# A fused Fourier, dense MoE and routed MoE kernel: one PSUM rotation, generators paced by TensorE's work, and a Fourier stage laid evenly over the chunks

## Chip, cores and metric

The kernel runs on one core of a Trainium2 chip. The metric is device time in microseconds (us), the median of several runs. Engines are named as in the profile: PE is TensorE, DVE VectorE, ACT ScalarE, POOL GpSimd, SP SyncE.

## The reference

Three stages follow each other: a filter in the frequency domain along the sequence, a gated MLP behind an RMS norm, and a top-1 mixture of experts. Eight batches of 3072 tokens with 256 features.

```python
def _attn_ref(x, w_r, w_i, b_r, b_i):
    X = np.fft.rfft(x, axis=1)
    Yr = Xr @ w_r - Xi @ w_i + b_r
    Yi = Xr @ w_i + Xi @ w_r + b_i
    Yr = np.sign(Yr) * np.maximum(np.abs(Yr) - lam, 0.0)   # Yi likewise
    return np.fft.irfft(Yr + 1j * Yi, n=x.shape[1], axis=1)
...
def _moe_ref(x, w_gate, w_val, w_out, rms_g):
    xn = x / np.sqrt(np.mean(x * x, axis=-1, keepdims=True) + 1e-06) * rms_g
    g = xn @ w_gate
    return (g * (1.0 / (1.0 + np.exp(-g))) * (xn @ w_val)) @ w_out      # d_ff 1536
...
def _moe2_ref(x, expert_emb, tau, w1, w2):                               # 8 experts, F 1024
    logits = normed(x) @ normed(expert_emb).T / tau
    expert_idx = np.argmax(logits, axis=1)
    # gate_w: the softmax of the logits at that expert
    out[mask] = gate_w[mask, None] * (np.maximum(x[mask] @ w1[e], 0.0) @ w2[e])
```

## The kernel before

The 24,576 tokens are cut into 64 chunks of 384 tokens, eight (c0 to c7) in each of eight batches. There are four stages: a start with the Fourier stage of batch 0 and the weights' preparation; seven batches whose chunks carry, in between, the Fourier stage of the next batch; batch 7, which carries the preparation of expert weights instead; and `phase_C`, the routed experts. Products are made of fp16 pairs (a high and a low part), three matmuls for one.

The work of a chunk is two runs of matmuls on PE. First, `gv` (L870) makes twelve gate and value tiles: for each f, six matmuls of 384 columns into a gate tile and six into a value tile (L879). ACT takes Silu of the gate tile into `th`, DVE multiplies it with the value tile into `hf`, which is then split into `hh` (ACT) and `hl` (DVE). Second, `out_tile` (L905) makes three output tiles of 36 matmuls with 264 columns (L913); the last 8 columns are routing logits.

Three other strands are written as Python generators, and calls in `gv` and in the main loop place their steps between these matmuls:

- `norm_steps` (L808) for the next chunk: 24 matmuls (L819) of the last Fourier step from `gt`, which was loaded from DRAM; squares on ACT; sums `q`, `q`, `ql` on POOL; a sum over features on PE (L839); a Newton reciprocal root on DVE; and `xnh`, `xnl`. `tick` takes one step at each call.
- `route_steps` (L928) for the chunk before: argmax, a prefix count on PE (L967, L969), positions, three scatters of row numbers `idl` by indirect DMA on POOL (L984), gate weights (`d`, `se`, `gw`), and a row written to DRAM.
- `gen_A` (L377), the Fourier stage of the next batch. In its A half 16 groups of twelve matmuls (L436) make `A`, a group every few steps. Then `A` is transposed by DMA into `at` (L482, issued by SP), which DVE scales (`level`). In the B half come 12 groups of sixteen (L511, into `c`), 24 of twelve (L540, into `yv`, `yw`, `yl`) and 24 of three (L558, into `go`, stored to `G`). `pump` hands out steps against a credit of 0.2 for each us of gate work and 0.6 for each us of output work.

The eight PSUM banks are split by `self.banks`: four for `gv` and the output tile k=1, one for the output tiles k=0 and 2, and three, named `ms`, for everything else. A tile takes the next bank of its name in turn, and the first matmul waits until the bank's earlier tile has been read. The build may place an instruction of DVE, ACT, POOL or SP earlier or later than it is written where dependences allow; PE keeps the written order; on the chip each engine works its queue in order.

Of the kernel before, what the change touches and what calls it, by code (L numbers as in the profile page):

```python
# [8 lines left out]
F32 = mybir.dt.float32  # L9
# [32 lines left out]

class Kern:
    def __init__(self, ctx, tc, ins, out):
# [20 lines left out]
    def msps(self, b, shape=(P, 512)):  # L65
        if b == 0:
            tag = self.rtags[self.rot % len(self.rtags)]
            self.rot += 1
        else:
            tag = "ms"  # L70
# [110 lines left out]
    def setup_A(self, pa, wp):  # L181
# [30 lines left out]
        ps = self.ps("ms")  # L212
# [164 lines left out]
    def gen_A(self, b):  # L377
# [49 lines left out]
        for step in range(NCH + 3):  # L427
            c = step - 3
            if c >= 0:
                xh, xl = hl.pop(c)  # L430
                for dc in range(2):
                    ps = self.msps(b, (P, 4, T1))
                    for t in range(4):
                        a = [z[:, t, dc * P:(dc + 1) * P] for z in (xh, xl)]
                        for j, (u, w) in enumerate(((0, 0), (0, 1), (1, 0))):
                            nc.tensor.matmul(ps[:, t], lhsT=a[u], rhs=self.d1[w], start=(j == 0), stop=(j == 2))  # L436
                    src = ps.rearrange("p t (l r) -> p l r t", r=2)
# [60 lines left out]
        for step in range(NPAIR + S3):  # L498
            if step < NPAIR and step % 2 == 0:
# [4 lines left out]
                level(i + 1)  # L504
# [3 lines left out]
                for l in range(4):  # L508
                    for dc in range(2):
                        for u in range(2):  # L510
                            nc.tensor.matmul(o[:, l // 2, dc, :, l % 2], lhsT=t[:, l, dc * P:(dc + 1) * P], rhs=self.c2[:, 4 * q + l, u], start=(u == 0), stop=(u == 1))  # L511

# [17 lines left out]
                yield 0.47  # L530
            if 2 <= step < NPAIR + 2:
# [21 lines left out]
            if step >= S3:  # L553
# [3 lines left out]
                for j, (u, w) in enumerate(((0, yh), (1, yh), (0, yl))):  # L557
                    nc.tensor.matmul(ps, lhsT=self.c3[:, g, u], rhs=w, start=(j == 0), stop=(j == 2))  # L558
                self.store_G(G, g, ps, 2.0 ** -10)
# [146 lines left out]
    def gen_wo(self, wp):  # L706
# [56 lines left out]
        for j in range(NF + 2):  # L763
            if j < NF:
                wt = wp.tile([P, 2, P], F32, tag="wot", name="wot", bufs=2)
                for k in range(2):
                    ps = self.ps("ms")
# [4 lines left out]
            if 1 <= j <= NF:  # L772
                wt = wts.pop(j - 1)
                ps = self.ps("ms")
# [28 lines left out]
    def load_gt(self, b, c):  # L803
        t = self.pb.tile([96, 4, 512], F16, tag="gt", name="gt", bufs=1)
# [3 lines left out]
    def norm_steps(self, b, c):  # L808
# [5 lines left out]
        for dc in range(2):  # L814
            ps = self.ps("ms", (P, 512))
            for t in range(4):
                a = [gt[:, t, h * D + dc * P:h * D + dc * P + P] for h in range(2)]
                for j, (u, w) in enumerate(((0, 0), (0, 1), (1, 0))):
                    nc.tensor.matmul(ps[:, t * T1:(t + 1) * T1], lhsT=a[u], rhs=self.d4[w], start=(j == 0), stop=(j == 2))  # L819
            self.act(v[:, dc], ps[:, 0:CT])  # L820
# [799 lines left out]
```

## Time and profile before

| what | us |
|---|---|
| median of 3 runs | 4161.88 (4154.77 to 4169.11) |
| the profiled execution | 4153.01 |
| its span | 4151.2 |
| start | 0 to 155.2 |
| main stage, batches 0 to 6 | 155.2 to 2771.1 |
| main stage, batch 7 | 2771.1 to 3073.3 |
| experts (`phase_C`) | 3073.3 to 4151.2 |
| busy: PE 3980.2, DVE 2763.4, ACT 1938.4, POOL 1225.7 | 96%, 67%, 47%, 30% of the span |

The times are read from one profiled execution, whose span lies 1.8 us under its own time. Batches 1 to 6 repeat each other, so batch 2 (899.4 to 1271.9) is read closely in what follows. PE's matmuls overlap in the trace: the time a group takes is the distance of its first start from the start of what follows it, not the sum of the durations.

### The profile page before, as it was taken

To read this page: it belongs to the slowest core of one execution; us is meant where nothing else is said; L and a number is where in the kernel's file an instruction comes from. 1 tells how busy PE (TensorE), PEld (TensorE's weight loads), DVE (VectorE), ACT (ScalarE), POOL (GpSimd) and SP (SyncE) were. 2 spreads that over 40 slices of the span, in tenths; PEclk is the share of its full clock that TensorE was granted. 3 is DMA by queue.
4 is the path that set the end of the run, shared out by engine and by line. 5 is a ranking of instruction groups with operands and counts; after the bars stand their busy time and mean duration, and the time that the engine had idled before them with its cause. 6 is when DMAs were issued, how large, how long until landed. Compare 5 with 4: busy or idle time off the path is not lost. (4 is left out here: it accounts for less than half of the span.)

```text
span 4151.2 us, 81518 instructions
## 1 busy us (share of the span) xinstructions
PE 3980.2 (96%) x31150; PEld 2821.6 (68%) x31150; DVE 2763.4 (67%) x7617; ACT 1938.4 (47%) x4326; POOL 1225.7 (30%) x1451
## 2 busy tenths in 40 slices
PE   8889999999999899999999998999999999999998
PEld 6567676766676677676766676766666666766666
DVE  7777787777778777876787787777854344343422
ACT  5544564455446445544554554445533333333432
POOL 3123213322322331232123213322233333333432
PEclk9899999999999999999999999999999999999999
DMA  7321022112101210211121112200024443343431
GB/s 230 88 51 45 24 51 54 36 32 57 48 28 47 57 44 24 60 47 34 36 56 42 31 34 52 80 24 24 20 56 135 94 115 95 77 109 92 84 76 42
DMA packets 324542, 252.57 MB, mean 61 GB/s; under 512 B 226294, under 2 KB 291108, under 8 KB 324147
## 3 DMA queue, kind: packets, MB, share of 16 engines
q1 hardware_dynamic: 298802, 195.60, 18.8%
q0 software_dynamic: 25344, 51.73, 4.8%
q8 instruction: 245, 4.01, 0.4%
q14 instruction: 151, 1.23, 0.1%
HBM read 120.64 MB, written 79.38 MB: 48 GB/s over the span
## 5 line engine op out<-in xcount | busy, mean ns | idle before, releaser
L879 PE MATMUL gv<-xnh,wgvh 128*128 128x384 f16 x3072 | 1013.2, 330 | 48.2 <-DVE hf L154 40.5
L879 PE MATMUL gv<-xnl,wgvh 128*128 128x384 f16 x3072 | 1012.4, 330 | 1.7 <-POOL xnl L150 1.7
L879 PE MATMUL gv<-xnh,wgvl 128*128 128x384 f16 x3072 | 1012.5, 330 | 0.0
L879 PEld LDWEIGHTS <-wgvh 128*128 128x128 f16 x6144 | 592.4, 99 | 444.2 <-issue 91.6
L158 ACT ACTIVATE hh<-hf 128x384 f16<-128x384 f32 x768 | 400.6, 522 | 696.4 <-DVE hf L154 687.1
L150 DVE TENSOR_TENSOR hl<-hf,hh 128x384 f16<-128x384 f32 x768 | 470.1, 612 | 161.6 <-ACT hh L158 158.5
L913 PEld LDWEIGHTS <-hh 128*128 128x128 f16 x4608 | 450.6, 98 | 72.0 <-ACT hh L158 2.3
L1150 PE MATMUL gv<-xt,w1h 128*128 128x512 f16 (+1 forms) x1664 | 482.2, 373 | 8.9 <-DVE el L154 8.9
L154 DVE SCALAR_TENSOR_TENSOR hf<-gv,kh,th 128x384 f32<-128x384 f32 x768 | 467.9, 609 | 33.8 <-PE gv L879 23.1
L158 ACT ACTIVATE th<-gv,kg 128x384 f32<-128x384 f32 x768 | 435.5, 567 | 112.0 <-PE gv L879 111.2
L154 DVE SCALAR_TENSOR_TENSOR el<-gv,eh 128x512 f16<-128x512 f32 (+1 forms) x416 | 276.7, 668 | 268.0 <-ACT eh L158 267.5
L879 PEld LDWEIGHTS <-wgvl 128*128 128x128 f16 x3072 | 302.4, 98 | 208.1 <-issue 12.3
L913 PE MATMUL out<-woh,hl 128*128 128x264 f16 x1536 | 425.1, 277 | 3.3 <-DVE hl L150 3.2
L913 PE MATMUL out<-woh,hh 128*128 128x264 f16 x1536 | 425.1, 277 | 1.2 <-ACT hh L158 1.1
L913 PE MATMUL out<-wol,hh 128*128 128x264 f16 x1536 | 425.1, 277 | 0.0
L158 ACT ACTIVATE eh<-gv 128x512 f16<-128x512 f32 (+1 forms) x416 | 240.6, 580 | 284.4 <-PE gv L1150 283.7
L1166 PEld LDWEIGHTS <-eh 128*128 128x128 f16 x3200 | 313.7, 98 | 56.8 <-issue 0.8
L1172 POOL DMA_INDIRECT out<-o,xg x200 | 202.9, 1015 | 502.6 <-ACT o L158 211.1
L1150 PE MATMUL gv<-xt,w1l 128*128 128x512 f16 (+1 forms) x832 | 310.6, 373 | 0.0
L984 POOL DMA_INDIRECT idl<-rowi,posi x192 | 208.2, 1085 | 320.6 <-DVE se L144 142.0
L150 POOL TENSOR_TENSOR xnl<-v,xnh 128x384 f16<-128x384 f32 x128 | 117.0, 931 | 567.8 <-ACT xnh L158 564.5
L1150 PEld LDWEIGHTS <-w1h 128*128 128x128 f16 x1664 | 163.2, 98 | 154.2 <-issue 12.5
(339 smaller groups left out, 7684.7 us busy)
## 6 DMA issues: line engine op xcount, KB each, us to landing
x2d<-row SPq DMA_DIRECT2D x64, 387.0 KB, 5.9
G<-go SPq DMA_DIRECT2D x192, 128.0 KB, 1.7
gt<-G SPq DMA_DIRECT2D x64, 384.0 KB, 4.4
xc<-in_x SPq DMA_DIRECT2D x60, 384.0 KB, 4.6
w1f<-in_moe_w SPq DMA_DIRECT2D x12, 1024.0 KB
w2f<-in_moe_w SPq DMA_DIRECT2D x12, 1024.0 KB, 6.2
xt<-xg SPq DMA_TRANSPOSE x200, 3.1
out<-o,xg POOLq DMA_INDIRECT x200
```

The lines of the kernel that those rows point to most:

```text
L150: (eng or self.nc.vector).tensor_tensor(out=out, in0=a, in1=b, op=op)
L154: self.nc.vector.scalar_tensor_tensor(out=out, in0=a, scalar=s, in1=b, op0=op0, op1=op1)
L158: self.nc.scalar.activation(out=out, in_=a, func=func, **kw)
L879: nc.tensor.matmul(p_, lhsT=self.wgv[q][u][:, dc, f * P:(f + 1) * P], rhs=xn[w][:, dc], start=(k == 0), stop=(k == 5))
L913: nc.tensor.matmul(ps, lhsT=a[:, k * P:(k + 1) * P], rhs=w[:, f], start=(n == 0), stop=(n == 3 * NF - 1))
L984: nc.gpsimd.indirect_dma_start(out=self.idl[k], out_offset=bass.IndirectOffsetOnAxis(ap=pi[:, k:k + 1], axis=0), in_=ri[:, k:k + 1], in_of ...
L1150: nc.tensor.matmul(ps, lhsT=w1[1 + a][:, dc, f * P:(f + 1) * P], rhs=xt[:, 2 * z + dc, 0:n], start=(k == 0), stop=(k == 5))
L1166: nc.tensor.matmul(ps, lhsT=a[:, f, k * P:(k + 1) * P], rhs=w2[1 + z][:, f], start=(j == 0), stop=(j == 3 * NFE - 1))
L1172: nc.gpsimd.indirect_dma_start(out=self.out, out_offset=bass.IndirectOffsetOnAxis(ap=xg[:, k, 257:258], axis=0), in_=o, in_offset=None, bo ...
```

## The change

One PSUM rotation: six banks named `s` serve gate, value, Fourier, norm, routing and expert hidden tiles in turn; two named `out` serve output tiles alone. `self.clk` counts PE's work in us, as constants of the code have it. The generators of norm and routing are wrapped in `Timed`: a step is taken once `clk` has passed the due time that the step before it named, and routing steps are 1.5 us apart in the gate run. The norm begins at f == 4, not at f == 2 (f == 6 in c7). One generator runs through the Fourier stages of all batches, and `due` says how much of it is to be done at each place: batch 1 by 6.65 chunks, and then one batch for every eight chunks (`TOTAL` = 80 units for a batch). `gt` has two buffers and is loaded two chunks ahead. Silu is written into `hf` itself, and `th` is gone. `hh` and `hl` go through two queues, `high` and `low`. `level(i + 1)` moves out of the L511 step into the step after it. `x2` has two buffers, `row` one. Line numbers move: L436 to L459, L511 to L534, L540 to L566, L558 to L585, L819 to L847, L839 to L864, L879 to L914, L913 to L950, L967 to L1003.

```diff
-        self.banks = {"gv": 4, "out": 1, "ms": 3}
+        self.banks = {"s": 6, "out": 2}
...
-        self.rtags = ("ms", "gv", "ms", "gv", "out", "ms", "gv", "gv")
+        self.rtags = ("s", "s", "s", "out")
...
+class Timed:
+    def __init__(self, g=()):
+        self.g, self.due, self.live = iter(g), 0.0, True
+
+    def step(self, clk):
+        if self.live and clk >= self.due:
+            d = next(self.g, None)
+            if d is None:
+                self.live = False
+            else:
+                self.due = clk + d
...
     def tick(self):
 
         next(self.xs, None)
-        a = next(self.ns, 0)
         if self.rate:
+            next(self.ns, None)
             self.rcred += self.rate
+            while self.rcred >= 1:
+                self.rcred -= 1
+                next(self.rs, None)
         else:
-            self.rcred = 1 if a else 2
-        while self.rcred >= 1:
-            self.rcred -= 1
-            next(self.rs, None)
+            self.ns.step(self.clk)
+            if self.clk >= self.rnext:
+                self.rs.step(self.clk)
+                self.rnext = self.clk + self.rgap
...
                 load(i + 2)
-                level(i + 1)
                 t = At.pop(q)
...
+            if step < NPAIR and step % 2 == 1:
+                level(step // 2 + 1)
             if 2 <= step < NPAIR + 2:
...
     def load_gt(self, b, c):
-        t = self.pb.tile([96, 4, 512], F16, tag="gt", name="gt", bufs=1)
+        t = self.pb.tile([96, 4, 512], F16, tag="gt", name="gt", bufs=2)
...
             self.act(v[:, dc], ps[:, 0:CT])
             self.act(q[:, dc], ps[:, 0:CT], AF.Square)
-            yield 1
-            yield 1
+            yield 1.0
         self.tt(q[:, 0], q[:, 0], q[:, 1], ALU.add, nc.gpsimd)
-        for _ in range(3):
-            yield 1
+        yield 1.0
...
         self.tt(q[:, 1], q[:, 0], qh[0], ALU.subtract, nc.gpsimd)
-        for _ in range(2):
-            yield 1
+        yield 1.0
         self.tt(ql, q[:, 1], qh[1], ALU.subtract, nc.gpsimd)
-        for _ in range(6):
-            yield 1
-
-        ps = self.ps("ms")[:, 0:CT]
+        yield 5.0
+
+        ps = self.ps("s")[:, 0:CT]
...
-            p_ = self.ps("gv")[:, 0:CT]
+            p_ = self.ps("s")[:, 0:CT]
...
-        t = pb.tile([P, CT], F32, tag="th", name="th", bufs=2)
-        self.act(t, ps[0], AF.Silu, scale=self.kg)
-        if self.hpend:
-            hl, h, hh = self.hpend
-            self.act(hh, h)
+        self.clk += 1.95
+        h = pb.tile([P, CT], F32, tag="hf", name="hf", bufs=3)
+        self.act(h, ps[0], AF.Silu, scale=self.kg)
+        self.high(1)
         self.tick()
-        h = pb.tile([P, CT], F32, tag="hf", name="hf", bufs=3)
-        self.stt(h, ps[1], self.kh, t, ALU.mult, ALU.mult)
-        self.flush_hl()
+        self.stt(h, ps[1], self.kh, h, ALU.mult, ALU.mult)
         self.tick()
+        self.low(1)
...
-        ps = self.ps(("out", "gv")[k % 2])[:, 0:264]
+        ps = self.ps("out")[:, 0:264]
...
         if k == 0:
-            for _ in self.rs:
-                pass
...
-            self.x2 = self.pr.tile([P, 3, 264], F32, tag="x2", name="x2", bufs=1)
+            self.x2 = self.pr.tile([P, 3, 264], F32, tag="x2", name="x2", bufs=2)
...
-        for _ in range(5):
-            yield
-
-        ps = self.ps("ms")
+        yield 5.0
+
+        ps = self.ps("s")
...
-        rw = pb.tile([P, 3, ROW], I32, tag="row", name="row", bufs=2)
+        rw = pb.tile([P, 3, ROW], I32, tag="row", name="row", bufs=1)
...
-            ps = self.ps("gv")[:, 0:n]
+            ps = self.ps("s")[:, 0:n]
...
-            ps = self.ps(("out", "ms")[k % 2])[:, 0:D]
+            ps = self.ps("out")[:, 0:D]
...
+        def due(i, share):
+
+            t = i + share
+            edge = NCH - 1.35
+            if t < edge:
+                return lead + (1 - lead) * t / edge
+            return 1 + (t - edge) / NCH
+
+        def pump(i, share, forced=None):
+            want = due(i, share) if forced is None else forced
+            while self.abatch - 1 + self.adone / TOTAL < want:
+                if next(ga, 0) == 0:
                     next(ge, None)
                     break
...
-                if more and edge and f == 3:
-                    drain(ga)
-                    self.load_gt(*chunks[i + 1])
-                if more and f == (6 if edge else 2):
-                    self.ns = self.norm_steps(*chunks[i + 1])
+                if f == 4 and i + 1 < n:
+                    self.ns = Timed(self.norm_steps(*chunks[i + 1]))
+                if f == 6 and i + 2 < n and c != NCH - 2:
+                    self.load_gt(*chunks[i + 2])
                 self.gv(b, c, f)
-                pump(1.95 * rg)
-            self.flush_hl(True)
+                share += 1.95 * GV / unit
+                pump(i, share)
+            self.high(1)
+            self.rgap = 0.0
             for k in range(3):
-                for x in self.out_tile(b, c, k):
+                if k == 2 and c == NCH - 2 and i + 2 < n:
+                    pump(i, share, b + 1)
+                    self.load_gt(*chunks[i + 2])
+                for j, x in enumerate(self.out_tile(b, c, k)):
+                    if j == 0:
+                        self.low(1)
                     self.tick()
...
-            drain(self.ns)
-            drain(self.rs)
-            self.rs = self.route_steps(b, c)
+            self.ns.drain()
+            self.rs.drain()
+            self.rs = Timed(self.route_steps(b, c))
```

Three places show how instructions move on the engines that PE waits for. The first is POOL in chunk c4 of batch 2. `q` and `ql` are the sums of the norm of c5, `idl` the scatters of the routing of c3, `rowi` the next row numbers, `yw` and `yl` belong to the Fourier stage. Before:

```order
L150 TENSOR_TENSOR yw<-yv,yw 128x256
L984 DMA idl_1245<-rowi,posi 211200x1
L984 DMA idl_1246<-rowi,posi 211200x1
L984 DMA idl_1247<-rowi,posi 211200x1
L959 TENSOR_SCALAR rowi<-kr 128x3
L150 TENSOR_TENSOR q<-q 128x384 x2
L150 TENSOR_TENSOR ql<-q 128x384
```

And in the changed kernel:

```order
L1046 TENSOR_SCALAR row<-kr 128x3
L173 TENSOR_TENSOR q<-q 128x384
L173 TENSOR_TENSOR yl<-yw,yh 128x256
L173 TENSOR_TENSOR q<-q 128x384
L173 TENSOR_TENSOR ql<-q 128x384
L173 TENSOR_TENSOR yw<-yv,yw 128x256
L1020 DMA idl_1245<-rowi,posi 211200x1
L1020 DMA idl_1246<-rowi,posi 211200x1
L1020 DMA idl_1247<-rowi,posi 211200x1
L996 TENSOR_SCALAR rowi<-kr 128x3
```

The norm's three sums moved ahead of the scatters and of `rowi`.

The second is DVE in chunk c3 of batch 2, where `go` (a tile of L558) and `yv` (of L540) are read out of PSUM; `d`, `se`, `gw` and `row` are the gate weights of the routing, `pos` the positions that follow L967. Before:

```order
L154 SCALAR_TENSOR_TENSOR d<-d,den 128x24
L1020 TENSOR_REDUCE se<-d 128x3
L144 TENSOR_SCALAR se<-se 128x3
L1025 RECIPROCAL gw<-se 128x3
L150 TENSOR_TENSOR gw<-gw,nrm 128x3
L144 TENSOR_SCALAR row<-gw,ko 128x3
L154 SCALAR_TENSOR_TENSOR go<-ms,go 128x256
L154 SCALAR_TENSOR_TENSOR yv<-ms,k_14033,bsc_14029 128x256
L150 TENSOR_TENSOR pos<-ms,cntb 128x24
```

And in the changed kernel:

```order
L169 TENSOR_SCALAR den<-d 128x24
L177 SCALAR_TENSOR_TENSOR go<-s,go 128x256
L1051 RECIPROCAL den<-den 128x24
L173 TENSOR_TENSOR hl<-hf,hh 128x384
L177 SCALAR_TENSOR_TENSOR d<-d,den 128x24
L1056 TENSOR_REDUCE se<-d 128x3
L167 TENSOR_SCALAR se<-se 128x3
L177 SCALAR_TENSOR_TENSOR hf<-s,kh,hf 128x384
L1061 RECIPROCAL gw<-se 128x3
L173 TENSOR_TENSOR gw<-gw,nrm 128x3
L167 TENSOR_SCALAR row<-gw,ko 128x3
```

`go` now stands ahead of the gate weights, whose steps are spread among `hf` and `hl`; `pos` follows 18 rows later.

The third is DVE in chunk c2 of batch 2, at the start of the B half, where the first three transposed tiles `at` are scaled. Before:

```order
L150 TENSOR_TENSOR hl<-hf,hh 128x384
L144 TENSOR_SCALAR at<-at,eq 128x1024
L154 SCALAR_TENSOR_TENSOR hf<-gv,kh,th 128x384
L144 TENSOR_SCALAR at<-at,eq 128x1024 x2
L150 TENSOR_TENSOR hl<-hf,hh 128x384
```

And in the changed kernel:

```order
L177 SCALAR_TENSOR_TENSOR hf<-s,kh,hf 128x384
L167 TENSOR_SCALAR at<-at,eq 128x1024 x2
L173 TENSOR_TENSOR hl<-hf,hh 128x384
L167 TENSOR_SCALAR at<-at,eq 128x1024
L177 SCALAR_TENSOR_TENSOR hf<-s,kh,hf 128x384
```

The three `at` stand within four rows in both.

## Rows read from the trace of the kernel before

**Rows 1.** The profile's page, busy time of each engine, share of the span, and number of instructions.

```profile
PE 3980.2 (96%) x31150; PEld 2821.6 (68%) x31150; DVE 2763.4 (67%) x7617; ACT 1938.4 (47%) x4326; POOL 1225.7 (30%) x1451
```

**Rows 2.** Windows by stage: batches 0 to 6, batch 7, the experts. Columns: stretch, its length, busy us (and instructions) of PE, PE's weight loads, DVE, ACT, POOL, granted clock of PE, DMA share, GB/s.

```profile
155.20:2771.10 2615.90, 2504.12 (x21033) 1806.36 (x21033) 1999.17 (x5695) 1318.72 (x3095) 718.39 (x894) 0.99 0.18 44
2771.10:3073.30 302.20, 298.92 (x2243) 207.77 (x2241) 221.46 (x639) 152.78 (x354) 74.05 (x85) 0.99 0.12 30
3073.30:4151.20 1077.90, 1051.91 (x7322) 716.75 (x7320) 429.89 (x971) 382.58 (x703) 387.18 (x391) 0.99 0.37 91
```

**Rows 3.** Windows of batch 2, the same columns: the batch, then its chunks c0, c1, c2, c3, c4 and c5.

```profile
899.40:1271.90 372.50, 356.95 (x3019) 258.13 (x3017) 285.79 (x821) 190.44 (x446) 102.26 (x128) 0.99 0.18 44
...
899.40:941.20 41.80, 41.22 (x373) 29.50 (x371) 36.16 (x111) 29.39 (x62) 8.78 (x10) 1.00 0.25 58
941.20:985.40 44.20, 43.01 (x400) 30.62 (x396) 40.63 (x137) 29.07 (x66) 8.13 (x10) 1.00 0.21 55
985.40:1048.30 62.90, 55.67 (x505) 41.06 (x503) 44.64 (x129) 25.73 (x65) 19.23 (x24) 0.97 0.27 54
1048.30:1106.40 58.10, 54.08 (x472) 40.39 (x470) 44.58 (x114) 26.07 (x63) 21.14 (x26) 0.97 0.19 53
1106.40:1160.30 53.90, 51.37 (x434) 38.39 (x433) 38.67 (x103) 25.49 (x63) 20.78 (x28) 1.00 0.17 41
1160.30:1197.50 37.20, 37.20 (x285) 26.06 (x284) 27.26 (x78) 18.43 (x44) 8.11 (x10) 1.00 0.10 29
```

**Rows 4.** Waits of PE in batches 0 to 6 (155.2 to 2771.1): who waits, what was awaited, us in total, times, longest.

```profile
PE gv L879 <- DVE hf L154: 38.1, 42, 3.0
PE ms L967 <- DVE go L154: 18.6, 6, 3.1
PE ms L839 <- POOL q L150: 17.6, 15, 2.3
PE ms L511 <- DVE c L154: 7.9, 6, 1.3
PE ms L540 <- ACT q L158: 6.2, 6, 1.5
PE ms L839 <- POOL ql L150: 5.8, 12, 0.6
PE ms L511 <- DVE at L144: 5.5, 2, 5.3
PE gv L879 <- ACT xnh L158: 3.9, 1, 3.9
PE out L913 <- DVE hl L150: 3.2, 5, 0.7
```

**Rows 5.** Timeline of PE in batch 2, four groups of Fourier matmuls, each with the matmul that follows the group. Columns: start, us, engine, line, operation, out<-in, tile, type, count.

```profile
923.26 0.25 PE L436 MATMUL ms<-kh,xh 96*128 96x96 f16 x2
...
923.77 0.33 PE L879 MATMUL gv<-xnh,wgvh 128*128 128x384 f16 x1
...
1004.82 0.63 PE L511 MATMUL ms<-c,at 128*128 128x64 f16 x16
1005.28 0.33 PE L879 MATMUL gv<-xnh,wgvh 128*128 128x384 f16 x1
...
1090.52 0.38 PE L558 MATMUL ms<-yh,c 128*128 128x256 f16 x2
...
1090.85 0.28 PE L913 MATMUL gv<-woh,hh 128*128 128x264 f16 x1
...
1091.53 0.38 PE L540 MATMUL ms<-wh,c 128*128 128x256 f16 x2
...
1092.84 0.28 PE L913 MATMUL gv<-woh,hh 128*128 128x264 f16 x1
```

**Rows 6.** Timeline of PE in c3 of batch 2, the routing's first matmul; in brackets the idle time before it and what ended it.

```profile
1061.14 0.18 PE L967 MATMUL ms<-oh,kh 128*128 128x32 f16 x1 [3.09 <-DVE go L154]
```

**Rows 7.** Timeline of DVE just before that matmul.

```profile
1059.89 0.88 DVE L144 TENSOR_SCALAR row<-gw,ko 128x3 f32<-128x3 f32 x1
1060.68 0.41 DVE L154 SCALAR_TENSOR_TENSOR go<-ms,go 128x256 f16<-128x256 f32 x1
```

**Rows 8.** Window of 3.41 us that begins 0.58 us ahead of that matmul; the 0.50 is the granted clock of PE.

```profile
1060.56:1063.97 3.41, 2.83 (x13) 1.42 (x13) 2.95 (x10) 0.54 (x1) 1.33 (x3) 0.50 0.45 155
```

**Rows 9.** Timelines of POOL and, in the last row, of PE, in c4 of batch 2.

```profile
1126.78 0.23 POOL L959 TENSOR_SCALAR rowi<-kr 128x3 int32<-128x3 int32 x1 [6.25 <-DMA idl<-rowi,posi]
1127.08 1.90 POOL L150 TENSOR_TENSOR q<-q 128x384 f32<-128x384 f32 x2
...
1128.13 0.33 PE L839 MATMUL ms<-q,onesb 128*128 128x384 bf16 x1 [1.39 <-POOL q L150]
```

**Rows 10.** Timelines of SP's queue, of DVE and of PE at the start of the B half of batch 2 (c2).

```profile
987.06 8.01 SPq L482 DMA_TRANSPOSE at<-A  x6
...
992.07 0.48 DVE L144 TENSOR_SCALAR at<-at,eq 128x1024 f16<-128x1024 f16 x1 [1.45 <-DMA at<-A]
...
996.27 0.49 DVE L144 TENSOR_SCALAR at<-at,eq 128x1024 f16<-128x1024 f16 x1 [1.99 <-DMA at<-A]
...
998.26 0.32 PE L879 MATMUL gv<-xnh,wgvh 128*128 128x384 f16 x1 [2.41 <-DVE hf L154]
```

**Rows 11.** Timeline of DVE in c0 of batch 2: the operation that empties the bank of the L436 group of the fifth group of rows.

```profile
926.67 0.55 DVE L150 TENSOR_TENSOR A<-ms,A 128x384 f16<-128x384 f32 x1
```

More of the change, by code (lines that the diff above doesn't have):

```diff
@@ L40, with drain @@
 LEAST = 2.0 ** -15 * 1.125
+class Timed:
[8 more added lines that the diff above has]
+                self.due = clk + d
+    def drain(self):
+        for _ in self.g:
+            pass
+        self.live = False
 class Kern:
@@ L69, in msps @@
         else:
-            tag = "ms"
+            tag = "s"
         return self.ps(tag, shape)
@@ L541, in gen_A @@
                             k += 1
+                self.clk += 1.3
                 self.tick()
@@ L773, in gen_wo @@
                 wt = wts.pop(j - 1)
-                ps = self.ps("ms")
+                ps = self.ps("s")
                 for k in range(2):
@@ L867, in norm_steps, with one @@
         self.xn[b, c] = (xh, xl)
-        yield 1
+        yield 0.0
+    def one(self, g):
+        while True:
+            try:
+                next(g)
+            except StopIteration as e:
+                return e.value
+            yield 0.0
     def gv(self, b, c, f):
@@ L914, in out_tile @@
                 n += 1
+            self.clk += 0.34
             if f < NF - 1:
@@ L1390, in main @@
         chunks = [(b, c) for b in range(self.NB) for c in range(NCH)]
-        ga, ge = iter(()), iter(())
-        self.load_gt(0, 0)
-        if self.NB > 1:
-            self.pend_x = self.load_x(1, 0)
-            ga = self.gen_A(1)
-            for _ in range(6):
-                next(ga)
-        self.ns = self.norm_steps(0, 0)
-        for _ in self.ns:
-            pass
-        credit = 0.0
-        rg, ro = 0.2, 0.6
-        def pump(cost):
-            nonlocal credit
-            credit += cost
-            while credit > 0:
-                x = next(ga, None)
-                if x is None:
-                    credit = 0.0
+        n = len(chunks)
@@ new lines, in main, with fourier @@
+        TOTAL = 80.0
+        self.abatch, self.adone = 1, 0.0
+        def fourier():
+            for b in range(1, self.NB):
+                self.pend_x = self.load_x(b, 0)
+                for x in self.gen_A(b):
+                    self.adone += x
+                    yield
+                self.abatch, self.adone = b + 1, 0.0
+        ga, ge = fourier(), iter(())
+        self.ns, self.rs = Timed(), Timed()
+        self.load_gt(0, 0)
+        self.load_gt(0, 1)
+        for _ in range(6):
+            next(ga, None)
@@ new lines, in main @@
+        for _ in self.norm_steps(0, 0):
+            pass
+        lead = self.adone / TOTAL
+        def due(i, share):
[8 more added lines that the diff above has]
+                if next(ga, 0) == 0:
@@ L1412, in pump @@
                     next(ge, None)
                     break
-                credit -= x
-        def drain(g):
-            for _ in g:
-                pass
+        GV, OUT = 0.2, 0.6
+        unit = NF * 1.95 * GV + 36 * 0.34 * OUT
         for i, (b, c) in enumerate(chunks):
             last = b == self.NB - 1
-            if c == 0:
-                if not last:
-                    if b:
-                        self.pend_x = self.load_x(b + 1, 0)
-                        ga = self.gen_A(b + 1)
-                        credit = 0.0
-                else:
-                    es.close()
-                    self.pw = ctx.enter_context(tc.tile_pool(name="pw", bufs=1, side="right"))
+            if last and c == 0:
+                es.close()
+                self.pw = ctx.enter_context(tc.tile_pool(name="pw", bufs=1, side="right"))
@@ L1440, in main @@
                 ge = self.gen_expert(self.pw, w1)
[L1441 to L1444 removed]
+            share = 0.0
+            self.rgap = 1.5
             for f in range(NF):
[L1446 to L1450 removed]
+                if f == 4 and i + 1 < n:
+                    self.ns = Timed(self.norm_steps(*chunks[i + 1]))
+                if f == 6 and i + 2 < n and c != NCH - 2:
+                    self.load_gt(*chunks[i + 2])
                 self.gv(b, c, f)
[L1452 to L1453 removed]
+                share += 1.95 * GV / unit
+                pump(i, share)
+            self.high(1)
+            self.rgap = 0.0
             for k in range(3):
[L1455 to L1464 removed]
+                if k == 2 and c == NCH - 2 and i + 2 < n:
[4 more added lines that the diff above has]
+                        self.low(1)
+                    self.tick()
+                    share += 0.34 * OUT / unit
+                    pump(i, share)
+            self.ns.drain()
+            self.rs.drain()
+            self.rs = Timed(self.route_steps(b, c))
+        self.rs.drain()
+        for _ in ge:
+            pass
         pbs.close()
```

115 lines of the change are left out of this document (57 added, 58 removed).

## The prediction

> **What bounds the kernel now.** I read the busy shares first [rows 1]: TensorE works 96% of the span, the next engine, VectorE, 67%. So the end is set by TensorE, and only its idle time and its slow clock can be won. The windows by stage [rows 2] say where that is: of the main stage with Fourier work (batches 0 to 6, 2615.9 us) TensorE is idle 111.8 us; batch 7, with no Fourier work, takes 302.2 us with 3.3 idle; the expert stage has 26.0 idle of 1077.9. The windows by chunk [rows 3] show the pattern inside a batch: a chunk without Fourier work takes 37.2 us, all busy, while c2, c3 and c4 of batch 2 take 62.9, 58.1 and 53.9 and hold 13.8 of the batch's 15.6 idle us.
>
> How much is there to win? The Fourier work of a batch, run without a stall, comes from the starts of its groups of matmuls and of what follows them [rows 5]: 16 groups of L436 at 0.51, 12 of L511 at 0.46, 24 of L558 at 0.33, 24 of L540 at 1.31: 8.2 + 5.5 + 7.9 + 31.4 = 53.0 us. With eight chunks of 37.2 a batch can't take less than 350.6; batch 2 took 372.5 [rows 3]. Over seven batches the floor is 2454.5 of 2615.9, so the **pot is 161 us**. The table of TensorE's waits [rows 4] names 106.8 of it (its larger lines): 38.1 for `hf` to empty a gate or value bank, 32.7 for Fourier and routing tiles that wait for an `ms` bank (18.6 + 7.9 + 6.2), 23.4 for the norm's sums from GpSimd (17.6 + 5.8), 5.5 for `at`, 7.1 for `hl` and `xnh`. The clock is a further part: c2 and c3 read 0.97, so 0.03 of 62.9 and of 58.1 is 3.6 us a batch, 25 in seven. The last 29 carry no name; small waits, and idle that the modelled ends of the matmuls cover.
>
> **One bank pool and the new place of the routing.** Before, every Fourier, norm and routing tile turns through three banks. At 1061.14 L967 waits 3.09 us [rows 6] for a bank that still holds a `go` tile, and VectorE reaches that `go` at 1060.68, behind six operations of three columns, the last of which took 0.88 us [rows 7]. The order listings of both kernels put a number on the room: the matmuls between a tile's last one and the first of the tile that reuses its bank are worth as little as 1 us for tiles in `ms` before; after, with six banks in one rotation, nowhere under some 2.5 us, and mostly 24 to 30 gate matmuls, 4 us or more (a gate chunk of 37.2 us is 252 matmuls, 0.15 each, and fewer, longer ones in the gate part). The drain is known from a row: the L436 group that gives way at 923.77 [rows 5] is emptied by `A` at 926.67 + 0.55 [rows 11], 3.45 us later. That stands clear of most of the new distances. The listing also has `go` ahead of `se`, `gw` and `row` at that place, no longer behind them. I take **30 of the 32.7** (20 to 33; below, if the drain grows: the slower rival).
>
> **The norm's sums.** GpSimd runs its queue in order. Before, `q`, `q`, `ql` stand behind the three `idl` scatters and `rowi`, and `rowi` waits 6.25 us for a scatter to land; then `q`, `q` take 1.90, and TensorE has been waiting 1.39 at 1128.13 [rows 9]. In the new order `q`, `q`, `ql` stand ahead of the scatters, and the generator is paced by TensorE's work, 5 us between `ql` and its matmul. What is late next is then the routing, whose scatters nobody on TensorE waits for; behind `rowi` stand the `yw` and `yl` of the Fourier stage, and L558 needs them some groups later, as it does now. **20 of 23.4** (10 to 23).
>
> **Gate and value banks.** Four banks before: a gate bank is wanted again after 18 matmuls, some 2.9 us by the kernel's own 1.95 us for a tile of twelve; VectorE behind by a few operations shows as a wait for `hf`. After, six banks shared with the rest: 24 to 30 matmuls. One part does not go. At the start of the B half VectorE stands at `at` operations that wait for the transposes (1.45 and 1.99 us), because SyncE takes 8.01 us over six issues, and TensorE waits 2.41 behind it [rows 10]. The listing still has the three `at` close together there. I leave 2.4 us a batch, 17 in all: of 38.1 + 5.5 = 43.6, **26 are saved** (0 to 35).
>
> **Clock and unnamed.** The 3.41 us from the end of that 3.09 us wait on ran at a granted clock of 0.50 [rows 8], the lower of the two levels (1.2 GHz), so up to half of 3.41, 1.7 us, is lost behind each such wait. With most of the long waits gone, 18 of 25 come back (7 stay, one drop of 1 us in each batch; the ends are half of it, 13, and all 25). Of the 29 unnamed I take **14**, the share that goes with the waits (0 to 29).
>
> The rows show 0.50 behind a wait of 3.09 us, and 1.00 in c0, c1 and c4 with 0.6 to 2.5 us of idle in smaller pieces [rows 3, 8]. A rule of the Trainium skill speaks against this change: "TensorE: Matmul & The Clock Gate", section "A second HAM failure mode: psum-queue depth-cycling", says that a kernel which turns through PSUM banks each iteration, with small idle gaps between groups of matmuls, makes the clock swing between its two levels. The trace agrees with that rule of the Trainium skill only behind the long waits; by the rule the sum would come out at the clock rival's time below, by the rows at the forecast's.
>
> **Spreading the Fourier work.** The new planner gives each chunk about 10 of 80 units instead of 16 in the first five chunks and none in c5 to c7. TensorE's work stays the same. What moves is VectorE's load: batch 2 has 285.8 us of it [rows 3], and c5 uses 27.3 of 37.2 while c1 has 40.6 of 44.2. After, the 285.8 lie in a batch of some 358 us, 80%, evenly; that is the gain. The cost is that no chunk is free of Fourier work: c1, at 92%, took 44.2 against 37.2 plus seven or eight groups of 0.51, so 3 us were lost there with VectorE near full. I take **5 lost** over the whole stage for the chunks whose gate part is dense with VectorE work (0 to 56, the upper end below).
>
> **At nothing:** `gt` two chunks ahead and `x2` in two buffers (TensorE's table has no wait for either; in c6 the load for the next batch's first chunk stands on SyncE right behind the last stores of `go`, and is wanted some 10 us into c7); one `row` buffer (its store left a chunk, 37 us, earlier); the routing's drain at the chunk's end, not at the first output tile (by then the generator has run out); Silu in place (an operand's name; `hf` has three buffers, freed a tile and a half before they are wanted); the longer queue for `hh` and `hl` (7.1 us of waits for `hl` and `xnh`, kept); batch 7 (3.3 us idle); the expert stage, whose hidden tiles turn over six banks, not four (at most some of 26.0); the start.
>
> **Sum.** 30 + 20 + 26 + 18 + 14 − 5 = 103. On the profiled execution, 4153.0 − 103 = 4050. The median of the runs is 4161.88, 1.0021 times that execution, so the forecast is **4059 us**.
>
> **The rivals.**
> - *VectorE takes the place of the banks.* For: the 92% of c1 [rows 3], and the small operations stretched to 0.88 us beside GpSimd [rows 7], which stay. Against: c0 had 36.2 of 41.8 and only 0.6 idle. If each of the 56 chunks loses 1 us, as a third of what c1 lost, 4059 + 56 = 4115.
> - *Nearly everything goes.* If 30 of the pot of 161 stay, 4153 − 131 = 4022, 4031 in the median; if 7 stay, 4008.
> - *The clock swings in every chunk.* Each chunk with Fourier work has one drop of 1.7 us: 56 × 1.7 = 95 in place of the 7 left, 4059 + 88 = 4147. For: micro-idles of bank waits would now be everywhere. Against: c0, c1 and c4 read 1.00 with 0.6 to 2.5 us idle [rows 3]. It is what the Trainium skill's section on psum-queue depth-cycling would do here.
> - *The change doesn't do what it says.* The build reorders VectorE's instructions, and the waits are VectorE's lateness, not bank count. Then idle moves from c2 to c4 into all chunks and the pot stays: 4150 to 4165.
> - *Slower: one slow tile holds a gate bank.* In the shared rotation the next tile, of whatever kind, waits for the oldest bank. Before, a late `A` held only an `ms` bank; now it stops the gate tiles, and thus all of TensorE. It decides where a drain takes longer than the 4 to 5 us of the new distance; 3.45 was seen [rows 11]. If the 16 `A` and 12 L511 tiles of each batch come 1 us too late, 28 × 7 = 196, 4059 + 196 = 4255; the crossing to slower lies at 0.5 us for each.
>
> **How the numbers follow.** Forecast 0.58, VectorE 0.18, nearly everything 0.08, clock 0.04, no effect 0.06, slower 0.06. About 0.3% (12.5 us) is what a measurement of this kernel can tell from no change. Below 4149 are the first four: faster 0.88; same 0.06; slower 0.06. The terms' own ends, 20 + 10 + 0 + 13 + 0 − 5 = 38 at worst and 33 + 23 + 35 + 25 + 29 − 0 = 145 at best, would be 4124 and 4017; the range runs from 4008 to 4124 and leaves out the clock, no effect, slower and about half of the best case, 0.2.
>
> **What would show it.** Right: the chunks of a batch take 43 to 46 us each with little difference; L967 (now L1003) and L511 are gone from TensorE's waits; waits for `q` and `ql` under 4 us; `hf` waits of about 2.4 us left once a batch at the start of the B half; the granted clock 1.00 but there. Wrong: waits for `hf`, `A` or `go` in many short pieces in all chunks with VectorE over 85% busy; a clock under 0.98 outside the B half's start; or gate matmuls that wait for `A` or `c`, which would be the slower rival's mark.

## The result, and the profile after

The changed kernel takes 4051.81 us (median of 4 runs, 4049.49 to 4054.58), the kernel before 4161.51 in the same comparison (4 runs): a ratio of 0.9736, 95% interval 0.9718 to 0.9754. The profiled execution took 4054.58 us, 98.4 less than the one profiled before (4153.01), while the medians lie 109.7 apart; what follows is read from the two profiled executions. The page of the new one and its windows by stage follow (start, batches 0 to 6, batch 7, experts; columns as in [rows 2]):

```profile
span 4052.4 us, 81479 instructions
PE 3949.2 (97%) x31150; PEld 2816.0 (69%) x31150; DVE 2776.3 (69%) x7617; ACT 1923.2 (47%) x4326; POOL 1250.3 (31%) x1451
```

```profile
0.00:161.10 161.10, 122.53 (x508) 88.59 (x509) 107.78 (x299) 79.68 (x167) 45.66 (x82) 0.91 0.65 192
161.10:2679.80 2518.70, 2479.91 (x21082) 1803.90 (x21082) 2018.15 (x5708) 1314.76 (x3103) 741.58 (x893) 1.00 0.18 46
2679.80:2984.70 304.90, 297.70 (x2248) 207.75 (x2247) 223.44 (x653) 151.69 (x357) 72.92 (x84) 0.99 0.08 23
2984.70:4052.40 1067.70, 1049.08 (x7316) 715.74 (x7316) 426.94 (x957) 377.01 (x700) 390.12 (x395) 0.99 0.37 93
```

Batches 0 to 6 went from 2615.9 [rows 2] to 2518.7, 97.2 us less. The other three stages nearly cancel: the start is 5.9 longer (155.2 before), batch 7 2.7, the experts 10.2 shorter. Of the 97.2, TensorE's visible idle time is 73.0 (111.8 to 38.8); the granted clock went from 0.99 to 1.00. Batch 2 and its chunks c0 to c5:

```profile
889.60:1248.70 359.10, 354.56 (x3019) 257.86 (x3017) 289.47 (x821) 188.51 (x446) 107.26 (x128) 1.00 0.18 45
889.60:929.80 40.20, 39.77 (x336) 28.14 (x334) 31.68 (x94) 24.03 (x54) 7.56 (x9) 1.00 0.20 43
929.80:974.00 44.20, 41.67 (x359) 29.18 (x357) 34.42 (x122) 24.74 (x58) 9.86 (x12) 1.00 0.15 40
974.00:1020.80 46.80, 46.20 (x409) 33.84 (x407) 39.02 (x103) 20.91 (x51) 13.72 (x17) 1.00 0.23 55
1020.80:1067.80 47.00, 46.83 (x395) 34.57 (x394) 38.40 (x101) 22.46 (x56) 17.47 (x21) 1.00 0.21 43
1067.80:1116.90 49.10, 48.60 (x420) 36.06 (x419) 38.40 (x103) 23.30 (x58) 17.52 (x22) 1.00 0.21 48
1116.90:1163.70 46.80, 46.80 (x409) 34.82 (x408) 36.84 (x100) 22.96 (x56) 16.21 (x21) 1.00 0.08 26
```

Against [rows 3] the batch lost 13.4 us. The chunks now lie between 40 and 49, and c1, with 2.5 idle in pieces of at most 0.5, has the most idle time, though VectorE is busy there for 34.4 of 44.2 and no longer for 40.6. TensorE's waits in batches 0 to 6 (columns as in [rows 4]):

```profile
PE s L914 <- DVE hf L177: 9.9, 26, 1.0
PE s L914 <- ACT xnh L181: 8.8, 2, 8.1
PE s L566 <- DVE c L552: 6.3, 7, 4.6
PE s L847 <- ACT hf L181: 4.3, 9, 0.5
PE s L914 <- ACT hf L181: 3.5, 11, 0.5
...
PE s L914 <- DVE A L173: 2.2, 5, 0.8
...
PE s L534 <- DVE at L167: 0.4, 1, 0.4
```

The lines for L967 (now L1003), `q` and `ql` (L864) are gone. `hf` fell from 38.1 to 9.9, and the longest of those waits from 3.0 to 1.0. New are short waits of a norm or gate tile for the bank of another kind (L847 for `hf`, L914 for `A`): the common rotation's price, 6.5 us in the lines shown. Two long waits in the table are each in one place: the 8.1 us for `xnh` end where the stage begins and belong to the start, and the 4.6 us of L566 for `c` are in batch 0, where VectorE has just stood 2.33 us at an `at` (before, L511 waited 5.3 us for `at` there [rows 4]). At the start of the B half of batch 2 (SyncE's queue and VectorE, as in [rows 10]):

```profile
972.08 8.09 SPq L506 DMA_TRANSPOSE at<-A  x6
...
978.80 0.49 DVE L167 TENSOR_SCALAR at<-at,eq 128x1024 f16<-128x1024 f16 x1 [1.69 <-DMA at<-A]
980.10 0.49 DVE L167 TENSOR_SCALAR at<-at,eq 128x1024 f16<-128x1024 f16 x1 [0.81 <-DMA at<-A]
...
981.37 0.49 DVE L167 TENSOR_SCALAR at<-at,eq 128x1024 f16<-128x1024 f16 x1 [0.32 <-DMA at<-A]
```

VectorE still stands there, 2.8 us in three pieces (4.2 before, with the 0.7 between the two rows shown), but no wait of 2.4 us of TensorE follows. GpSimd in c4 of batch 2:

```profile
1089.97 0.84 POOL L173 TENSOR_TENSOR ql<-q 128x384 bf16<-128x384 f32 x1
...
1093.94 1.06 POOL L1020 DMA_INDIRECT idl<-rowi,posi  x1 [2.45 <-DVE posi L1018]
...
1102.80 0.85 POOL L996 TENSOR_SCALAR rowi<-kr 128x3 int32<-128x3 int32 x1 [4.97 <-DMA idl<-rowi,posi]
```

`rowi` still waits, 4.97 us against 6.25 in [rows 9], but `ql` has been done for 12 us.

### The profile page after: what moved, and what is told of

The parts are those of the page before. It is cut to its first block, busy times and chain, and to the rows that moved or that the text cites. A ratio compares the mean times of both kernels' runs of the same rounds, so it can differ in the third digit from the quotient of the medians.

```text
span 4052.4 us, 81479 instructions
## 1 busy us (share of the span) xinstructions
PE 3949.2 (97%) x31150; PEld 2816.0 (69%) x31150; DVE 2776.3 (69%) x7617; ACT 1923.2 (47%) x4326; POOL 1250.3 (31%) x1451
## 5 line engine op out<-in xcount | busy, mean ns | idle before, releaser
L914 PE MATMUL s<-xnh,wgvh 128*128 128x384 f16 x3072 | 1001.6, 326 | 26.4 <-DVE hf L177 9.9
L914 PE MATMUL s<-xnl,wgvh 128*128 128x384 f16 x3072 | 1001.4, 326 | 4.3 <-POOL xnl L173 4.0
L914 PE MATMUL s<-xnh,wgvl 128*128 128x384 f16 x3072 | 1001.8, 326 | 0.0
L914 PEld LDWEIGHTS <-wgvh 128*128 128x128 f16 x6144 | 588.9, 98 | 392.7 <-issue 41.2
L950 PE MATMUL out<-woh,hl 128*128 128x264 f16 x2304 | 636.0, 276 | 4.2 <-DVE hl L173 3.2
L950 PE MATMUL out<-woh,hh 128*128 128x264 f16 x2304 | 636.1, 276 | 0.3 <-ACT hh L181 0.3
L950 PE MATMUL out<-wol,hh 128*128 128x264 f16 x2304 | 636.0, 276 | 0.0
L950 PEld LDWEIGHTS <-hh 128*128 128x128 f16 x4608 | 450.8, 98 | 69.7 <-issue 0.9
L177 DVE SCALAR_TENSOR_TENSOR hf<-s,kh,hf 128x384 f32<-128x384 f32 x768 | 468.9, 611 | 32.9 <-PE s L914 11.5
L1186 PE MATMUL s<-xt,w1h 128*128 128x512 f16 (+1 forms) x1664 | 481.1, 372 | 5.3 <-DMA xt<-xg 2.5
L181 ACT ACTIVATE hf<-s,kg 128x384 f32<-128x384 f32 x768 | 434.4, 567 | 57.5 <-PE s L914 46.0
L914 PEld LDWEIGHTS <-wgvl 128*128 128x128 f16 x3072 | 300.1, 98 | 206.3 <-issue 8.1
L1202 PE MATMUL out<-w2h,el 128*128 128x256 f16 x1600 | 436.2, 273 | 2.5 <-DVE el L177 2.3
L1202 PE MATMUL out<-w2l,eh 128*128 128x256 f16 x1600 | 436.1, 273 | 0.0
L1202 PE MATMUL out<-w2h,eh 128*128 128x256 f16 x1600 | 436.1, 273 | 0.0
L1186 PE MATMUL s<-xt,w1l 128*128 128x512 f16 (+1 forms) x832 | 309.9, 372 | 1.1 <-issue 1.1
```

The source lines that it names most:

```text
L177: self.nc.vector.scalar_tensor_tensor(out=out, in0=a, scalar=s, in1=b, op0=op0, op1=op1)
L181: self.nc.scalar.activation(out=out, in_=a, func=func, **kw)
L914: nc.tensor.matmul(p_, lhsT=self.wgv[q][u][:, dc, f * P:(f + 1) * P], rhs=xn[w][:, dc], start=(k == 0), stop=(k == 5))
L950: nc.tensor.matmul(ps, lhsT=a[:, k * P:(k + 1) * P], rhs=w[:, f], start=(n == 0), stop=(n == 3 * NF - 1))
L1186: nc.tensor.matmul(ps, lhsT=w1[1 + a][:, dc, f * P:(f + 1) * P], rhs=xt[:, 2 * z + dc, 0:n], start=(k == 0), stop=(k == 5))
L1202: nc.tensor.matmul(ps, lhsT=a[:, f, k * P:(k + 1) * P], rhs=w2[1 + z][:, f], start=(j == 0), stop=(j == 3 * NFE - 1))
```

## The experiments

Theory A was the prediction's: the common rotation carries most of the gain, the norm's new place some 20 us. The rivals: the even spread, or the pacing, carries it. Each ratio is to the kernel before in the same set (medians 4149.4, 4155.6, 4163.7 and 4136.7 us in the four sets), five rounds, with its 95% interval. Where two kernels of different sets are compared, the ratios are compared and not the times.

**after_again**, the changed kernel unchanged. 

> The changed kernel once more, as the measure for kernels on the same chip: 0.9736 of the kernel before, between 0.972 and 0.976.

 Measured: 4053.86 us, 0.9754 (0.9741 to 0.9768). With 0.9736 above, 0.2% between sets is not an effect.

**split_banks**, the banks taken back:

```diff
-        self.banks = {"s": 6, "out": 2}
+        self.banks = {"gv": 4, "out": 1, "ms": 3}
```

> The changed kernel with the banks split as before: four for gate and value tiles and output tile k=1, one for output tiles k=0 and 2, three for all else; everything else is the change. Theory A (the common rotation of six banks is what removes the waits): the waits on ms and gate banks come back, 32.7 + 26 + some 14 of clock, so 4105 to 4130 us. Rival B (the even Fourier spread and the new pacing remove the waits, the bank count does nothing): 4050 to 4065 us, no line of PE for c, go or ACT q above 8 us.

 Measured: 4075.9 us, 0.9820 (0.9807 to 0.9834), 0.7 to 0.8% or some 30 us slower than the changed kernel: between the two theories. Its waits in the main stage:

```profile
PE gv L914 <- DVE hf L177: 21.7, 28, 2.5
PE gv L914 <- ACT hf L181: 13.0, 15, 1.5
PE ms L585 <- DVE go L177: 9.1, 13, 1.2
```

The gate waits come back in part; of the `ms` waits only 9.1 for `go` come, in pieces of up to 1.2 us and ahead of another tile (L585), and none for L1003.

**pool_only**, the kernel before with one rotation:

```diff
-        self.banks = {"gv": 4, "out": 1, "ms": 3}
+        self.banks = {"s": 6, "out": 2}
```

> The kernel before with one rotation of six banks and two output banks, and nothing else of the change. Theory A: the 32.7 us of ms waits and some 26 of the hf waits go, and part of the clock with them, while the norm's q and ql waits (23.4) stay: 4075 to 4100 us. Rival B: within 15 us of the kernel before, 4145 to 4165 us. Third case: a late c or A holds a gate bank while the Fourier groups stand close together, slower than 4165 us.

 Measured: 4123.7 us, 0.9934 (0.9920 to 0.9948), 26 us faster. Not within either forecast. Its waits, in a profiled execution of 4132.87 us:

```profile
PE s L879 <- DVE hf L154: 28.8, 15, 5.6
PE s L839 <- POOL q L150: 15.4, 14, 2.0
PE s L879 <- DVE go L154: 13.1, 6, 2.3
```

The L967 wait for `go` (18.6 in [rows 4]) is there again as a wait of a gate tile behind it: VectorE reaches `go` late in either kernel, and the rotation only passes the late bank on to another tile. The slower rival's mechanism is real, at up to 2.3 us a batch. The wait at the start of the B half is longer than before, not shorter. In batch 2 VectorE stands there for 4.3 us at the three `at` (1.90, 0.38 and 2.05), and the gate tile waits 3.59 where it waited 2.41 [rows 10]:

```profile
1008.15 0.32 PE L879 MATMUL s<-xnh,wgvh 128*128 128x384 f16 x1 [3.59 <-DVE hf L154]
```

Over batches 1 to 6 such waits come to 24.5 of the 28.8 us for `hf`. Six banks alone don't cover this stand.

**bunched**, the changed kernel with the old distribution of Fourier work:

```diff
-            t = i + share
-            edge = NCH - 1.35
...
+            t = (i % NCH + share) / 4.9
```

> The changed kernel with the Fourier work bunched as before, done in the first 4.9 chunks of a batch instead of evenly over eight. Theory A: a small loss, 4055 to 4075 us, since six banks cover the denser chunks too. Rival B (VectorE's even load is the gain): 4100 to 4140 us, with waits for hf, c and go in c2 to c4 and low-clock windows.

 Measured: 4051.85 us, 0.9771 (0.9757 to 0.9784): at most 0.4% slower than the changed kernel, and its interval overlaps that of after_again. The even spread isn't the gain. Two of its windows, c2 and c3 of batch 2, beside 62.9 and 58.1 in [rows 3]:

```profile
962.90:1019.70 56.80, 53.60 (x482) 39.80 (x480) 44.13 (x128) 25.02 (x61) 17.64 (x23) 0.97 0.27 57
1019.70:1074.00 54.30, 54.30 (x501) 41.64 (x500) 45.95 (x121) 27.05 (x69) 23.31 (x28) 1.00 0.21 59
```

c3 has VectorE at 85% and TensorE without a gap. In c2 a norm tile (L847) waits 2.04 us for `hf` and a gate tile, 2.2 us later, 1.10, and the clock fell there:

```profile
980.27:983.68 3.41, 3.37 (x11) 1.62 (x11) 2.49 (x7) 3.13 (x7) 1.00 (x1) 0.50 0.58 143
```

In batches 1 to 6 four such drops come, each at the start of the B half; the changed kernel has none in these batches.

**norm_ticks**, the norm one step at each tick, beginning at f == 2:

```diff
-            self.ns.step(self.clk)
+            next(self.ns.g, None)
```

> The changed kernel with the norm's generator taken one step at each tick with the old counts, beginning at f == 2 (f == 6 in c7), as before; banks, Fourier spread and routing as changed. Theory A: PE's waits for q and ql come back, about 15 to 23 us, so 4065 to 4078 us. Rival C (with six banks and fewer Fourier steps in the way the old pacing does as well): 4045 to 4058 us, q and ql waits under 5 us.

 Measured: 4091.41 us, 0.9858 (0.9843 to 0.9873), 1.0 to 1.2% slower than the changed kernel, over 40 us. But not by `q` and `ql`. Its first line of waits, and GpSimd and TensorE at one such place:

```profile
PE s L585 <- POOL yl L173: 25.1, 7, 4.7
```

```profile
1204.94 0.97 POOL L1024 DMA_INDIRECT idl<-rowi,posi  x1 [0.30 <-DMA idl<-rowi,posi]
1205.93 0.97 POOL L173 TENSOR_TENSOR yl<-yw,yh 128x256 f16<-128x256 f32 x1
1210.53 0.23 POOL L1000 TENSOR_SCALAR rowi<-kr 128x3 int32<-128x3 int32 x1 [3.64 <-issue]
...
1213.15 1.29 POOL L173 TENSOR_TENSOR yl<-yw,yh 128x256 f16<-128x256 f32 x2
...
1213.86 0.37 PE L585 MATMUL s<-yl,c 128*128 128x256 f16 x1 [4.38 <-POOL yl L173]
```

Here `rowi`, behind the scatters, stands ahead of a Fourier `yl` instead of `q`; two `xnl` and a `yw` stand between them, so `yl` begins 2.4 us after `rowi` ends. The profile names no releaser for these 3.64 us ("issue"); over the stage it puts most of the idle time before `rowi` down to the scatters (119.1 of 136.7 us). The granted clock fell behind that wait:

```profile
1213.40:1216.80 3.40, 2.94 (x14) 2.02 (x14) 1.10 (x4) 1.32 (x5) 1.04 (x2) 0.56 0.33 116
```

That made a new theory D: what costs is `rowi`, which waits until a scatter has landed and holds up whatever stands behind it on GpSimd. Four kernels keep the row numbers in one tile that is filled at the start (not shown), so that this step is gone from the loop:

```diff
-        ri = self.sm(pb, "rowi", 3, I32)
-        nc.gpsimd.tensor_scalar(out=ri, in0=self.krow, scalar1=float(r0), scalar2=None, op0=ALU.add)
+        if r0 // CT == 32:
+            nc.gpsimd.tensor_scalar(out=self.rall, in0=self.rall, scalar1=float(32 * CT), scalar2=None, op0=ALU.add)
+        ri = self.rall[:, r0 // CT % 32]
```

**before_rows**: 

> The kernel before, with the scatters' row numbers kept in one tile of 32 chunks that is filled at the start and raised once in the middle, so that no rowi step stands on GpSimd behind the scatters. Theory D (rowi's wait for a scatter to land is what makes q and ql late): PE's waits for q and ql fall from 23.4 us to under 8, and the time by 15 to 30 us. Rival E (GpSimd is late by its own work, or q's place behind the scatters' issue is what counts): waits for q and ql above 15 us and a gain under 8 us.

 Measured: 4125.13 us, 0.9929 (0.9916 to 0.9943), 30 us faster. Of the 23.4 us of waits for `q` and `ql` 0.9 are left, and the first lines read:

```profile
PE gv L880 <- DVE hf L154: 45.4, 43, 3.3
PE ms L979 <- DVE go L154: 18.6, 6, 3.1
```

**norm_ticks_rows**: 

> The changed kernel with the norm by ticks, as in norm_ticks, and the same kept row numbers. Theory D: the one long wait a batch for yl (25.1 us in seven batches) and the low clock behind it go, so 30 to 40 us less than norm_ticks, within 15 us of the changed kernel. Rival E: less than 15 us off, yl waits above 12 us.

 Measured: 4063.25 us, 0.9776 (0.9762 to 0.9791), 0.8% or some 34 us under norm_ticks by the ratios. Waits for `yl` fall from 25.1 to 9.6, so `rowi` was most of them and not all.

**after_rows**: 

> The changed kernel with the same kept row numbers. Theory D: rowi's waits there hold up nothing that TensorE waits for, so within 6 us of the changed kernel; if some of the short waits in c7, c0 and c1 come from GpSimd, up to 12 us faster.

 Measured: 4054.15 us, 0.9756 (0.9740 to 0.9772), as after_again. Theory D holds in all three: the new place of the norm gains, in the main, what taking `rowi` away gains, and after it `rowi` costs nothing.

**pool_rows**, the kernel before with both edits: 

> The kernel before with both single edits: the common rotation of six banks and two, and the kept row numbers. If the two gains are apart (0.66% and 0.71%): a ratio of 0.985 to 0.988, which leaves about 1.1% for the pacing, level and spread. If they remove the same waits: 0.990 or more. If they help each other, 0.982 or less.

 Measured: 4108.0 us, 0.9871 (0.9856 to 0.9886). The two gains add up, 1.3% of 2.5%.

**route_ticks**, the routing by ticks, drained at the first output tile:

```diff
-            if self.clk >= self.rnext:
-                self.rs.step(self.clk)
-                self.rnext = self.clk + self.rgap
+            for _ in range(1 if self.ns.live else 2):
+                next(self.rs.g, None)
```

> The changed kernel with the routing's generator taken by ticks as before (one step at a tick, two when no norm is under way, drained at the first output tile); banks, norm and Fourier as changed. Theory F (the routing's pacing, which spreads the gate-weight steps and puts go ahead of them, is the third part of the gain beside banks and norm): waits for go of 10 us or more come back on PE, 15 to 30 us slower than the changed kernel, a ratio of 0.979 to 0.983 to the kernel before. Rival G (with six banks the place of go does not matter): 0.973 to 0.977.

 Measured: 4059.99 us, 0.9749 (0.9735 to 0.9762). No slower beyond the intervals; theory F falls. Waits for `ql` and `q` (9.9 and 6.5) take the place of others, and none for `go` comes. But in this kernel `go` never stands right behind the gate weights on VectorE either, so it doesn't test what that order is worth.

**level_old**, `level` in its old place:

```diff
                 load(i + 2)
+                level(i + 1)
...
-            if step < NPAIR and step % 2 == 1:
-                level(step // 2 + 1)
```

> The changed kernel with level(i + 1) written in the L511 step again, as before. If the new place is what took the wait for at and the first hf wait of the B half away: 2 to 3 us a batch, 14 to 20 us slower, a ratio of 0.978 to 0.981. Otherwise (the build puts the first three at together in both): 0.973 to 0.977.

 Measured: 4054.74 us, 0.9736 (0.9723 to 0.9750). No effect.

**all_paces**, the diffs of norm_ticks, route_ticks, bunched and level_old at once. 

> The changed kernel with every pacing as before at once: norm and routing by ticks, routing drained at the first output tile, Fourier work bunched into 4.9 chunks, level in the L511 step. What stays of the change: the six banks, Silu in place, the queues for hh and hl, and the buffers of gt, x2 and row. Theory H (the part of the gain that no single edit explains is pacing, whose parts stand in for each other): as pool_only, a ratio of 0.990 to 0.996 to the kernel before. Rival I (Silu in place and the queues for hh and hl carry some 30 us): 0.982 to 0.988.

 Measured: 4062.52 us, 0.9817 (0.9804 to 0.9831). Theory H falls: with every pacing as before, 1.8% of the gain is there. It is faster than norm_ticks, though it undoes more, so the long `yl` wait there is no cost of ticks as such. That it came from the new routing pace meeting the old norm's is likely but not shown, since the spread and `level` differ too. Its waits for `q` and `ql` are 7.7 us:

```profile
PE s L916 <- ACT hf L180: 14.3, 18, 3.3
PE out L952 <- DVE hl L172: 11.4, 23, 0.7
...
PE s L866 <- POOL ql L172: 5.5, 7, 0.8
```

From pool_only (0.9934) to all_paces (0.9817) lie 1.2%, some 48 us. What differs is Silu in place, the queues for `hh` and `hl`, the buffers of `gt`, `x2` and `row`, `gt` two chunks ahead, and the form of the Fourier planner. No run parts these. The two traces say which waits went, though not which edit took them: those at the start of the B half (24.5 us in pool_only; in batches 1 to 6 of all_paces none over 0.4), `go` (13.1 to 0.9), `q` and `ql` (19.7 to 7.7). Others came, 14.3 for ACT's `hf` above all. In sum TensorE's idle time in batches 0 to 6 fell from 94.7 to 56.6 us, and its granted clock rose from 0.98 to 1.00. The part for `q` and `ql` is one that pool_rows wins too. For `go` the traces show more. In pool_only, as before [rows 7], it stands right behind the last gate weight (`row`); in all_paces it stands ahead of them:

```profile
1069.05 0.88 DVE L144 TENSOR_SCALAR row<-gw,ko 128x3 f32<-128x3 f32 x1
1069.84 0.41 DVE L154 SCALAR_TENSOR_TENSOR go<-s,go 128x256 f16<-128x256 f32 x1
```

```profile
1045.96 0.42 DVE L176 SCALAR_TENSOR_TENSOR go<-s,go 128x256 f16<-128x256 f32 x1
...
1051.77 1.75 DVE L166 TENSOR_SCALAR row<-gw,ko 128x3 f32<-128x3 f32 x1
```

Over the main stage that order occurs six times in the kernel before, in pool_only, before_rows and pool_rows, and each of these has six waits for `go` (18.6, 13.1, 18.6 and 13.2 us). It occurs once, in batch 0, in all_paces and never in the changed kernel, split_banks and route_ticks, and none of these has a wait for `go` of more than 1.2 us.

## Why the prediction was right, and where its terms were not

- **What bounds the kernel.** Right: TensorE's idle time and its clock in batches 0 to 6. The forecast took 103 us there, 97.2 went; 4059 stood against 4051.81.
- **The `ms` banks (30 of 32.7).** The waits went, but the rotation is not what took most of them. By pool_only and split_banks the rotation is worth 26 to 30 us in all, where the prediction hung 30 + 26 and part of the clock on it. In pool_only 13.1 of the 18.6 for `go` are back at a gate tile, and new waits for `c` and `q` (3.0, 1.7 and 3.5) stand for the old ones (7.9 and 6.2). The forecast's second reason, `go` ahead of the gate weights, fits every trace: the long waits for `go` come where it stands right behind them and nowhere else. No run changes this order alone, so it is not shown as the cause. The rival that called the waits VectorE's lateness and not a matter of bank count was right on these. (Of the six small operations ahead of `go`, five have three columns and `d` has 24.)
- **The norm's sums (20 of 23.4).** Right in mechanism and size: no such wait is left, and before_rows shows that `rowi`'s wait was the cause (30 us with the clock behind it). The new order is not the only cure: all_paces keeps `rowi` and the ticks and has 7.7.
- **Gate and value banks (26 of 43.6).** About right in size: 9.9 for `hf` and 0.4 for `at` remain, and with 3.5 for ACT's `hf` and the 4.6 for `c` in batch 0 it is 18.4, so between 25 and 33 went. Wrong is the part that was to stay, 2.4 us at the start of each B half: in batches 1 to 6 no wait there is over 1.01. More banks alone don't explain it. With six banks and nothing else (pool_only) these waits are 3.6 to 5.6; with the other edits and four banks (split_banks) 1.1 to 2.5; in the changed kernel, with both, at most 1.01. VectorE's stand in batch 2 fell from 4.2 to 2.8 us. In batch 0, where 5.3 us were waited for `at`, the 4.6 for `c` stand in their place.
- **Clock and unnamed (18 + 14).** Of 97.2, 73.0 is visible idle, so 24.2 is the clock and idle hidden under modelled ends, against 32 in the sum (and 73.0 against the other terms' 71). In batches 0 to 6 of the kernel before, the trace has the clock at its lower level in fourteen stretches, 61.4 us in all (a stretch that begins in the start is left out in either kernel). At half the clock that cost at most half, 31 us, so the clock alone can account for all 24.2, and little of the unnamed 14 need have come. In the changed kernel one of 3.41 us is left, behind the 4.62 us wait for `c` in batch 0:

```profile
288.45:291.86 3.41, 3.41 (x17) 2.41 (x16) 1.09 (x3) 0.00 (x0) 0.02 (x1) 0.50 0.01 2
```

- **The clock rival.** The rule of the Trainium skill's "TensorE: Matmul & The Clock Gate", section "A second HAM failure mode: psum-queue depth-cycling", has no support in the changed kernel: with one rotation and idle of at most 2.5 us in a chunk, every chunk of batch 2 reads 1.00. Short waits are not harmless everywhere. In bunched, with the same rotation, the clock fell to 0.50 behind waits of 2.04 and 1.10 us, and in another batch behind 1.27 and 1.10.
- **Spreading (−5).** The price was about right (c0 and c1 idle 3.0 in batch 2, 1.8 before), but "that is the gain" was wrong: bunched shows none that can be measured. The chunks are less even than forecast, 40 to 49 us and not 43 to 46.
- **At nothing.** Wrong twice. The start is 5.9 longer: in pool_only it is 4.1 longer by the rotation alone, and there as here the first gate matmul waits 8.1 us for `xnh`, where it waited 3.9. The experts are 10.2 shorter (3.3 in the profile of after_again), with the waits for `el` down from 11.7 to 4.5. The rotation alone gives this too: pool_only has the experts at 1068.8 us, 9.1 less than before, and split_banks at 1082.9 with 17.0 us of waits for `el`. And among Silu in place, the queues, the buffers and the planner's form, all counted at nothing, lies the open 1.2%.

So the sum came out by errors that cancel: the total of the waits was right, since nearly all of them went, and what removed them was shared out wrongly. That it is this near is in part luck. Open is which of the small edits carries the 1.2%, and with it which one moves `go` ahead of the gate weights and shortens the wait at the start of the B half.

## What to carry to other kernels

A table of waits told well here how much could go, and poorly which edit takes it: the waits for banks were in large part a late reader, and more banks handed the wait to the next tile. Before you add banks, look at what the reader stands behind in its own queue. Look on each queue for an instruction that waits for a DMA and for what stands behind it; here a three-column `rowi` cost 0.7%. Where many strands meet, undo edits singly and together: here one undone alone (norm_ticks) cost more than four undone at once (all_paces).

## What was not expected of the hardware

An instruction that reuses a scatter's row numbers can stand for long: `rowi` waited 6.25 us [rows 9] and 4.97 for the scatters, whose issues took about 1 us each (3.64 in norm_ticks, where the profile names no releaser). In batches 0 to 6 of the changed kernel TensorE kept the upper clock level through waits of up to 1.01 us and lost it behind one of 4.62; with the Fourier work bunched it lost it behind two waits of 1.27 and 1.10 us, 2.2 us apart.
